# Two transformer layers on one core: the turned features' stores move from SyncE's queue to ScalarE's, one pipeline round later

## The chip, the cores and the metric

The kernel runs on one core of a Trainium2 chip. A core has TensorE (matrix products; PE in the profile), VectorE (DVE), ScalarE (ACT), GpSimd (POOL) and SyncE (SP), each with its own queue of instructions that it runs in order, and 16 DMA engines that move data between memory and the core. A transfer is begun by an instruction in one engine's queue: SP's or ScalarE's here. The metric is the device time of one execution in microseconds (us). The time of a kernel is the median of its runs; the profile is one execution, recorded by the hardware.

## The reference, cut to what matters

There are two layers, each an attention block A and a feed-forward block B, in float32, on 2048 rows of width 576, with 32 heads of 18 and a hidden width of 4608:

```python
def A(x):                                   # x is layer-normed, [1, 2048, 576]
    q, k, v = split_heads(x @ wqkv)         # [1, 32, 2048, 18] each
    pq, pk = (einsum("bhsd,hdf->bhsf", a, w_phi) for a in (q, k))
    phi_q = concat([softmax(pq), softmax(-pq)], -1)
    phi_k = concat([softmax(pk), softmax(-pk)], -1)
    kv = einsum("bhsf,bhsd->bhfd", phi_k, v)
    z = einsum("bhsf->bhf", phi_k)
    num = einsum("bhqf,bhfd->bhqd", phi_q, kv)
    den = einsum("bhqf,bhf->bhq", phi_q, z)[..., None] + 1e-6
    return merge_heads(num / den) @ wo

def B(x):                                   # x is layer-normed
    r = maximum(x @ w1 + b1, 0)
    return (r * r) @ w2 + b2

x = x + A(ln(x)); x = x + B(ln(x))
x = x + A(ln(x)); x = x + B(ln(x))
```

## The kernel before, in words

The rows are worked in four blocks of 512 (`TB`), and a block in four tiles of 128 rows (`NT` = 4). Every float32 product is made of three products of rounded parts (hi x hi, lo x hi, hi x lo), so each operand is split: ScalarE copies the rounded part, VectorE or GpSimd subtracts it.

In a layer, sums over all keys are made first; then the blocks go one after the other through query features, attention output and the feed-forward block. The feed-forward of one block (`g_mlp`, names m_0 to m_3 in the profile) fills TensorE and is the main thread. It takes 36 steps, one for each 128 of the hidden columns. A step f of it:

- `first` loads w1 for the step (three transfers on SP, L1159 and twice L244) and w2 (one, L1161), into two buffers each, and splits them: the copies are L1167 (w1) and L1168, L1169 (w2) on ScalarE, the subtractions L1171, L1174 on VectorE and L1175 on GpSimd.
- `hidden` is 14 matmuls into the tile ph (L1190).
- `square` is L1197 to L1199 on ScalarE (ReLU with the bias, and the square twice) and L1200 on VectorE.
- `second` for the step before, f - 1, is 12 matmuls (L1217) and 3 (L1208).

While this runs, the next blocks' attention is woven in. `weave(main, other, rate)` gives the other thread `rate` units after each step of the main one, and every step of the other thread yields its cost in units. The rate is 3.7 beside the first feed-forward block of a layer and 5.0 beside the second. `chained` orders the steps of the other thread on VectorE, ScalarE and GpSimd one behind the other, and `held` puts them behind the latest square (key "squared", L1199 on ScalarE) and the latest low part (key "last", L1200 on VectorE). Apart from such orders, the place of an instruction in its engine's queue is planned when the program is built.

The features of a block's queries are made in `g_features`, a pipeline over the four tiles: in round i stage k works on tile i - k, the last stage first. The stages are `start` (maximum and minimum, differences), the exponential (ScalarE, 1.15 us), `add` (sums, products with the key sums), `factors`, the scaling (VectorE and GpSimd), and `turn`, which turns 32 x 32 squares in place on VectorE (L897) and begins four transfers on SP (L900), one for each quarter of 32 partitions, to a DRAM tile `home` that holds the features by columns. A transfer moves 144 KB in runs of 32 numbers (128 bytes). Six calls are made in the run, three in each layer: they appear as tiles a_0Q0e to a_3Q3e and the DRAM tiles a_0ft to a_3ft.

`g_out` fetches the turned features back (`fetch`, L928 on SP, 504 KB for a group of heads), into buffers of the tag "E", of which there are four, the same that hold the feature tiles. ScalarE copies (L941) and VectorE subtracts (L942), and TensorE multiplies with the key sums (pn, L964). In four of the six calls another block's queries and features lie between `g_features` and its `g_out`. In the two others (tiles a_1, beside m_2, and a_2 in the second layer, beside m_0) `g_out` follows at once, behind a pause of 5.0 units.

Of the kernel before, what the change touches and what calls it, by code (L numbers as in the profile page):

```python
# [21 lines left out]
def layers_kernel(  # L22
# [18 lines left out]
    nc = tc.nc  # L41
# [77 lines left out]
    def pipeline(n, stages, costs):  # L119

        for i in range(n + len(stages) - 1):
            for k in reversed(range(len(stages))):
                if 0 <= i - k < n:
                    stages[k](i - k)
                    yield costs[k]
# [514 lines left out]
    def soft_parts(src, name, apart=False):  # L640
        if apart:
            e = sb.tile([P, 2 * D], F32R, tag="hb", name=f"{name}e").bitcast(F32)
            e = e.rearrange("p (s d) -> p s d", s=2)
        else:
            e = sb.tile([P, 2, D], F32, tag="E", name=f"{name}e", bufs=4)
        v = src.rearrange("p (h d) -> p h d", d=DH)
        mm = sb.tile([P, 2, H], F32, tag="mm", name=f"{name}m")
        nc.vector.tensor_reduce(mm[:, 0], v, op=ALU.max, axis=AX.X)
        nc.vector.tensor_reduce(mm[:, 1], v, op=ALU.min, axis=AX.X)
        e4 = e.rearrange("p s (h d) -> p s h d", d=DH)  # L650
        m = mm.unsqueeze(3).to_broadcast([P, 2, H, DH])
        dense["parted"] = nc.vector.tensor_sub(e4[:, 0], v, m[:, 0])
        dense["parted", 1] = nc.gpsimd.tensor_sub(e4[:, 1], m[:, 1], v)
        return e

    def soft_exp(e):
        return nc.scalar.activation(e, e, AF.Exp)

    def soft_sums(e, name):
        r = sb.tile([P, 2, H], F32, tag="r", name=f"{name}r", bufs=4)  # L660
        nc.vector.tensor_reduce(r, e.rearrange("p s (h d) -> p s h d", d=DH), op=ALU.add, axis=AX.X)
        nc.vector.reciprocal(r, r)
        return r
# [142 lines left out]
    def held(gen, keys=("last",)):  # L806

        while True:
            with ExitStack() as behind:
                for key in keys:  # L810
                    behind.enter_context(tc.issue_after(dense[key].ins))
                cost = next(gen, gen)
            if cost is gen:
                return
            yield cost
# [15 lines left out]
    def phi_products(layer, e, name):  # L831
        zb = sums[layer]["zb"]
        ms = [sb.tile([P, D], F32, tag="qk", name=f"{name}{s}", bufs=5) for s in range(2)]
        for s in range(2):
            (nc.gpsimd if s else nc.vector).tensor_mul(ms[s], e[:, s], zb[:, s])
        return ms

    def phi_sums(ms, name):
        u = sb.tile([P, 2, H], F32, tag="u", name=name)
        for s in range(2):  # L840
            nc.vector.tensor_reduce(u[:, s], ms[s].rearrange("p (h d) -> p h d", d=DH), op=ALU.add, axis=AX.X)
        return u

    def phi_factors(u, r):
        nc.vector.tensor_mul(u, u, r)
        nc.vector.scalar_tensor_tensor(u[:, 0], u[:, 0], DEN_EPS, u[:, 1], op0=ALU.add, op1=ALU.add)
        nc.vector.reciprocal(u[:, 1], u[:, 0])
        nc.vector.tensor_mul(r, r, u[:, 1].unsqueeze(1).to_broadcast([P, 2, H]))

    def phi_scale(e, r, which=(0, 1)):  # L850
        for s in which:
            e3 = e[:, s].rearrange("p (h d) -> p h d", d=DH)
            dense[f"scaled{s}"] = (nc.gpsimd if s else nc.vector).tensor_mul(
                e3, e3, r[:, s].unsqueeze(2).to_broadcast([P, H, DH]))
# [24 lines left out]
    def g_features(layer, raws, ph, name):  # L879

        rs, ms = {}, {}

        def start(t):
            ph.append(soft_parts(raws[t], f"{name}Q{t}"))

        def add(t):
            rs[t] = soft_sums(ph[t], f"{name}Q{t}")
            ms[t] = phi_products(layer, ph[t], f"{name}m{t}")

        def factors(t):  # L890
            phi_factors(phi_sums(ms.pop(t), f"{name}u{t}"), rs[t])

        turned[name] = home = dram.tile([2 * D, TB], F32, name=f"{name}ft")

        def turn(t):
            flat = ph[t].rearrange("p s d -> p (s d)")
            nc.vector.transpose(flat, flat)  # L897
            for i in range(NQ):
                at = t * P + 32 * i
                nc.sync.dma_start(home[:, at : at + 32].rearrange("(j f) r -> f j r", f=32),  # L900
                                  flat[32 * i : 32 * i + 32].rearrange("f (j r) -> f j r", r=32))

        yield from held(pipeline(NT, (start, lambda t: soft_exp(ph[t]), add, factors, lambda t: phi_scale(ph[t], rs[t]),
                                      turn), (2.6, 0.4, 3.0, 2.8, 1.2, 1.6)), ("last", "squared"))

    def g_out(layer, b, ph, dst, name, parts=1, pause=None, behind=None, norm=None, mid=None, costs=(None, None), o_first=None):

# [793 lines left out]
    def g_attend(layer, b, x, raws, dst, name, behind=None, norm=None, mid=(None, None), ph=None):  # L1701

        if ph is None:
            ph = []
            if raws is None:
                raws = []
                yield from g_queries(layer, b, x, raws, name)
            yield from g_features(layer, raws, ph, name)
        yield 5.0
        if mid[0]:  # L1710
            yield from mid[0]
        yield from g_out(layer, b, ph, dst, name, behind=behind and (behind["last"],), norm=norm, mid=mid[1],
                         costs=(1.0, None if norm else 3.0))
# [120 lines left out]
    for layer in range(2):  # L1834
# [5 lines left out]
        def back_first():  # L1840
            m, later = f"a{layer}_{order[2]}", []
            mid = (g_queries(layer, order[2], None, later, m), g_features(layer, later, early, m))
            yield from g_attend(layer, order[1], None, raws, nxt, f"a{layer}_{order[1]}", dense, None, mid)
# [142 lines left out]
```

## Time and profile before

| | us |
|---|---|
| median of 3 runs | 2439.97 |
| lowest and highest run | 2436.8 and 2958.45 |
| profiled execution | 2442.47 |
| its span in the trace | 2440.8 |
| TensorE busy | 2412.5 |
| VectorE busy | 1560.7 |
| ScalarE busy | 1290.9 |

The profiled execution's time is 1.7 us above its span: that much lies outside the first and last instruction. How to read the lines: "L900" is a line of the kernel; "x4" is a count of instructions; "out<-in" names the tiles written and read, with the numbers of the buffers left out; SPq is SP's queue, and a DMA_DIRECT2D there is the instruction that begins a transfer, whose duration is that of the beginning alone and not of the moving. Such instructions are not counted as busy time of an engine. In a timeline a row has the start, the duration and the engine, and in brackets how long the engine stood before it, and for whom. In a row of waits stand the total, the number and the longest. PEclk is the clock that TensorE was granted, as a share of full speed. The DMA share is the mean busy share of the 16 DMA engines; it can come out a little above 1. A matmul's duration overlaps that of the next: the pace is read from starts.

### The profile page before, as it was taken

Reading aid. Unit: us, or ns where it says so; the run is one execution under the profiler, and the core shown is the slowest. Engines: PE = TensorE matmul, PEld = TensorE weight load, DVE = VectorE, ACT = ScalarE, POOL = GpSimd, SP = SyncE. Lnnn points to the kernel's source line nnn. Section 1 sums busy time; section 2 is a strip of 40 time slices with the busy share of each in tenths; the row PEclk is TensorE's granted clock in tenths of the full one; section 3 lists DMA queues with packets and bytes.
Section 4 is the critical chain, followed back from the end, with each engine's and each line's share of the span. In section 5 each row is a group of like instructions: output and inputs, shape, how many; then the busy total and the mean of one; then the engine's idle time right before and its main releaser. Section 6 shows DMA issues by size and latency. Waiting matters only on the chain. (4 is left out here: it accounts for less than half of the span.)

```text
span 2440.8 us, 41473 instructions
## 1 busy us (share of the span) xinstructions
PE 2412.5 (99%) x14806; PEld 2140.8 (88%) x14806; DVE 1560.7 (64%) x2537; ACT 1290.9 (53%) x2543; POOL 939.9 (39%) x1121
## 2 busy tenths in 40 slices
PE   9999999999999999999999999999998999999999
PEld 8999888888788888888999988888887888888898
DVE  7778848664866655545766788486557675555443
ACT  4344555444446766664433445554455466676643
POOL 4555303222326565542433442032122455565321
PEclk9999999999999999999999999999999999999999
DMA  9124573756654533338753156637667444333364
GB/s 338 64 84 164 163 194 102 168 185 228 151 159 129 162 105 108 112 102 301 254 188 147 59 167 145 173 96 195 194 224 162 130 143 144 119 103 117 110 199 130
DMA packets 370646, 379.40 MB, mean 155 GB/s; under 512 B 142886, under 2 KB 270790, under 8 KB 367878
## 3 DMA queue, kind: packets, MB, share of 16 engines
q1 hardware_dynamic: 369180, 375.37, 51.3%
q8 instruction: 116, 1.90, 0.3%
q10 hardware_dynamic: 1258, 1.37, 0.2%
q14 instruction: 92, 0.75, 0.1%
HBM read 297.22 MB, written 79.41 MB: 154 GB/s over the span
## 5 line engine op out<-in xcount | busy, mean ns | idle before, releaser
L1508 POOL TENSOR_TENSOR m_ps<-m_pr,m_ps 128x128 fp32r<-128x128 f32 x144 | 98.8, 686 | 338.1 <-ACT m_ps L1506 310.9
L1507 DVE TENSOR_TENSOR m_ps<-m_pr,m_ps 128x448 fp32r<-128x448 f32 x144 | 99.8, 693 | 176.1 <-ACT m_ps L1505 176.0
L1550 PE MATMUL m_pacc<-m_ps,m_phb 128*128 128x448 f32 x864 | 185.6, 363 | 0.0
L1550 PEld LDWEIGHTS m_pacc<-m_ps,m_phb 128*128 128x128 f32 x864 | 161.9, 188 | 15.1
L1550 PE MATMUL m_pacacc<-m_ps,m_phc 128*128 128x448 f32 x648 | 147.1, 365 | 0.0
L1505 ACT ACTIVATE m_ps<-m_pr 128x448 fp32r<-128x448 f32 x144 | 82.8, 575 | 115.8 <-issue 66.6
L1550 PEld LDWEIGHTS m_pacacc<-m_ps,m_phc 128*128 128x128 f32 x648 | 119.2, 188 | 7.7
L1190 PE MATMUL m_2ph<-a_2nh,m_2h 128*128 128x512 f32 (+1 forms) x380 | 98.1, 385 | 1.9 <-ACT m_2h L1167 1.7
L1190 PE MATMUL m_0ph<-a_0nh,m_0h 128*128 128x512 f32 (+1 forms) x380 | 97.6, 383 | 1.8 <-ACT m_0h L1167 1.7
L1217 PE MATMUL m_2acc<-m_2s,m_2hb 128*128 128x448 f32 x432 | 95.4, 368 | 2.9 <-ACT m_2s L1168 2.6
L1217 PE MATMUL m_0acc<-m_0s,m_0hb 128*128 128x448 f32 x432 | 95.2, 368 | 2.9 <-ACT m_0s L1168 2.6
L1190 PE MATMUL m_1ph<-t1onh,m_1h 128*128 128x512 f32 (+1 forms) x380 | 95.8, 381 | 0.5 <-ACT m_1hr L1197 0.3
L1190 PE MATMUL m_3ph<-t0onh,m_3h 128*128 128x512 f32 (+1 forms) x380 | 95.7, 381 | 0.2 <-DVE t0onh L534 0.2
L1217 PE MATMUL m_3acc<-m_3s,m_3hb 128*128 128x448 f32 x432 | 93.6, 363 | 0.0
L1217 PE MATMUL m_1acc<-m_1s,m_1hb 128*128 128x448 f32 x432 | 93.5, 363 | 0.0
L1217 PEld LDWEIGHTS m_2acc<-m_2s,m_2hb 128*128 128x128 f32 x432 | 82.0, 191 | 11.7 <-ACT m_2s L1168 3.0
L1217 PEld LDWEIGHTS m_0acc<-m_0s,m_0hb 128*128 128x128 f32 x432 | 81.7, 190 | 11.6 <-ACT m_0s L1168 3.0
L1217 PEld LDWEIGHTS m_3acc<-m_3s,m_3hb 128*128 128x128 f32 x432 | 80.7, 188 | 7.9 <-DVE m_3hb L1200 0.4
L1217 PEld LDWEIGHTS m_1acc<-m_1s,m_1hb 128*128 128x128 f32 x432 | 80.7, 188 | 7.8 <-DVE m_1hb L1200 0.3
L1175 POOL TENSOR_TENSOR m_3s<-m_3r,m_3s 128x128 fp32r<-128x128 f32 x36 | 22.3, 620 | 158.2 <-ACT m_3s L1169 147.0
L1175 POOL TENSOR_TENSOR m_1s<-m_1r,m_1s 128x128 fp32r<-128x128 f32 x36 | 22.0, 612 | 156.7 <-ACT m_1s L1169 139.4
L1190 PEld LDWEIGHTS m_1ph<-t1onh,m_1h 128*128 128x128 f32 x380 | 68.8, 188 | 15.3 <-ACT m_1hr L1197 0.7
(2464 smaller groups left out, 7241.0 us busy)
## 6 DMA issues: line engine op xcount, KB each, us to landing
m_pr<-in_B_w SPq DMA_DIRECT2D x144, 288.0 KB
m_pr<-in_B_w SPq DMA_DIRECT2D x72, 256.0 KB
hd<-m_pu SPq DMA_DIRECT2D x72, 256.0 KB
m_pg<-hd SPq DMA_DIRECT2D x72, 256.0 KB
m_3r<-in_B_w SPq DMA_DIRECT2D x36, 288.0 KB
m_2r<-in_B_w SPq DMA_DIRECT2D x36, 288.0 KB
m_1r<-in_B_w SPq DMA_DIRECT2D x36, 288.0 KB
m_0r<-in_B_w SPq DMA_DIRECT2D x36, 288.0 KB
```

The costliest lines, as they stand in the source:

```text
L1175: nc.gpsimd.tensor_sub(s2[:, FC + P : FC + 2 * P], r2[:, R:], s2[:, FC : FC + P].bitcast(F32))
L1190: dense["hidden"] = nc.tensor.matmul(ph[:, cols], a, m, start=(k == 0), stop=(k == len(ops) - 1))
L1217: nc.tensor.matmul(acc[t][:, :R], a[:, rows], m, start=(f == 0 and k == 0), stop=(f == NF - 1 and k == 2))
L1505: nc.scalar.activation(s2[:, RO : RO + R], r2[:, :R], AF.Copy)
L1507: nc.vector.tensor_sub(s2[:, RO + R : RO + 2 * R], r2[:, :R], s2[:, RO : RO + R].bitcast(F32))
L1508: nc.gpsimd.tensor_sub(s2[:, FC + P : FC + 2 * P], r2[:, R:], s2[:, FC : FC + P].bitcast(F32))
L1550: nc.tensor.matmul(accs[b][t][:, :R], a[:, rows], m, start=(g == 0 and k == 0), stop=(g == NF - 1 and k == 2))
```

## The change

The stage `turn` keeps the turning on VectorE. A seventh stage `store` holds the four transfers, which are now begun by ScalarE's queue. Being the next stage of the pipeline, it works on a tile one round after the turning. The cost of the stage `turn`, 1.6 units, is divided into 1.4 and 0.2.

```diff
         def turn(t):
             flat = ph[t].rearrange("p s d -> p (s d)")
             nc.vector.transpose(flat, flat)
+
+        def store(t):
+            flat = ph[t].rearrange("p s d -> p (s d)")
             for i in range(NQ):
                 at = t * P + 32 * i
-                nc.sync.dma_start(home[:, at : at + 32].rearrange("(j f) r -> f j r", f=32),
+                nc.scalar.dma_start(home[:, at : at + 32].rearrange("(j f) r -> f j r", f=32),
                                   flat[32 * i : 32 * i + 32].rearrange("f (j r) -> f j r", r=32))
 
         yield from held(pipeline(NT, (start, lambda t: soft_exp(ph[t]), add, factors, lambda t: phi_scale(ph[t], rs[t]),
-                                      turn), (2.6, 0.4, 3.0, 2.8, 1.2, 1.6)), ("last", "squared"))
+                                      turn, store), (2.6, 0.4, 3.0, 2.8, 1.2, 1.4, 0.2)), ("last", "squared"))
```

## The prediction

> **What bounds the kernel now.** I read the page's table of engines first, then TensorE's own waits, then the timeline around the longest of them.
>
> ```profile
> span 2440.8 us, 41473 instructions
> PE 2412.5 (99%) x14806; PEld 2140.8 (88%) x14806; DVE 1560.7 (64%) x2537; ACT 1290.9 (53%) x2543; POOL 939.9 (39%) x1121
> ...
> q10 hardware_dynamic: 1258, 1.37, 0.2%
> ```
>
> TensorE is the bound: 28 us of the span are left idle. q10 is ScalarE's queue, almost unused (packets, MB, share). The waits of TensorE, longest first (total, times, longest; the first load is left out):
>
> ```profile
> PE m_2acc L1217 <- ACT m_2s L1168: 2.6, 1, 2.6
> PE m_0acc L1217 <- ACT m_0s L1168: 2.6, 1, 2.6
> PE a_1pn L964 <- ACT a_1fh L941: 2.0, 1, 2.0
> PE m_2ph L1190 <- ACT m_2h L1167: 1.7, 1, 1.7
> PE m_0ph L1190 <- ACT m_0h L1167: 1.7, 1, 1.7
> PE a_2pn L964 <- ACT a_2fh L941: 1.6, 1, 1.6
> ```
>
> They are two copies of one event, once in m_2 and once in m_0, where TensorE stands for copies of weights (L1168, L1167) and of turned features (L941). The timeline of m_0 (start, duration, engine):
>
> ```profile
> 1840.29 0.34 SPq L1161 DMA_DIRECT2D m_0r<-in_B_w  x1
> ...
> 1842.30 0.38 SPq L1159 DMA_DIRECT2D m_0r<-in_B_w  x1
> ...
> 1846.21 0.58 ACT L1168 ACTIVATE m_0s<-m_0r 128x448 fp32r<-128x448 f32 x1 [0.65 <-PE m_0acc L1208]
> ...
> 1847.45 0.80 DVE L1171 TENSOR_TENSOR m_0h<-m_0r,m_0h 128x640 fp32r<-128x640 f32 x1
> ...
> 1849.35 0.69 ACT L1197 ACTIVATE m_0hr<-m_0ph,b1t 128x512 f32<-128x512 f32 x1 [2.36 <-PE m_0ph L1190]
> 1849.55 0.68 DVE L1200 TENSOR_TENSOR m_0hb<-m_0hr,m_0hb 128x512 fp32r<-128x512 f32 x1
> ...
> 1852.25 1.31 PE L1190 MATMUL m_0ph<-a_0nh,m_0h 128*128 128x512 f32 x5
> ...
> 1854.41 2.31 SPq L900 DMA_DIRECT2D a_2ft<-a_2Q1e  x4
> ...
> 1855.43 2.57 PE L1217 MATMUL m_0acc<-m_0s,m_0hb 128*128 128x448 f32 x12
> ...
> 1856.82 0.61 SPq L1161 DMA_DIRECT2D m_0r<-in_B_w  x1
> ...
> 1858.54 1.31 PE L1190 MATMUL m_0ph<-a_0nh,m_0h 128*128 128x512 f32 x5
> ...
> 1861.45 1.38 DVE L897 STREAM_TRANSPOSE a_2Q3e<-a_2Q3e 128x1152 f32<-128x1152 f32 x1
> ...
> 1863.24 3.49 SPq L900 DMA_DIRECT2D a_2ft<-a_2Q3e  x4
> ...
> 1866.78 0.72 SPq L1159 DMA_DIRECT2D m_0r<-in_B_w  x1
> ...
> 1871.65 1.43 PE L1190 MATMUL m_0ph<-a_0nh,m_0h 128*128 128x512 f32 x5 [1.66 <-ACT m_0h L1167]
> ```
>
> A step of m_0 lasts 1858.54 - 1852.25 = 6.29 us, and each should load w2 (L1161) and w1 (L1159) once. Instead SP stands at the store L900 for VectorE's turning, and the next loads start 16.5 us (1840.29 to 1856.82) and 24.5 us (1842.30 to 1866.78) after the last. The copy at 1847.45 had freed the w1 buffer by 1848.25, so the load could have gone then. TensorE's next step starts after 1871.65 - 1858.54 = 13.11 us: 6.8 lost. The step behind it, in TensorE's own timeline:
>
> ```profile
> 1874.95 2.57 PE L1217 MATMUL m_0acc<-m_0s,m_0hb 128*128 128x448 f32 x12
> ...
> 1878.06 0.40 PE L964 MATMUL a_2pn<-a_2fh,kbh 126*126 126x512 f32 x1
> 1878.29 0.40 PE L964 MATMUL a_2pn<-a_2fh,kbl 126*126 126x512 f32 x1
> ...
> 1887.80 2.57 PE L1217 MATMUL m_0acc<-m_0s,m_0hb 128*128 128x448 f32 x12
> ```
>
> From 1874.95 to 1887.80 are 12.85 us for one step and twelve a_2pn matmuls at 0.23: 6.29 + 2.8 = 9.1 by rights, so 3.8 more are lost. Together 10.6 us in m_0. m_2 has the same waits and 0.4 more at L964: I take 11.0. That is 21.6 us in all, the most that this edit can win: in the other four calls of the feature pipeline TensorE does not wait.
>
> **The change, part by part.** *The stores leave SP.* 96 transfers (six calls, four tiles, four quarters). What SP stood there for (total, times, longest), and what the DMA engines did meanwhile (columns: five engines, clock, DMA share, GB/s):
>
> ```profile
> SPq L900 <- DVE a_0Q1e L897: 20.4, 2, 10.7
> ...
> SPq L900 <- DVE a_2Q1e L897: 16.0, 2, 9.7
> ...
> SPq L900 <- DVE a_1Q1e L897: 8.0, 1, 8.0
> ...
> SPq L244 <- DMA a_2w<-a_2ft: 4.0, 3, 2.0
> ```
>
> ```profile
> core 0: us, PE busy (x) PEld busy (x) DVE busy (x) ACT busy (x) POOL busy (x), PEclk, DMA share, GB/s
> 1846.00:1856.00 10.00, 10.00 (x47) 8.57 (x46) 9.90 (x16) 3.61 (x7) 3.92 (x3) 1.00 0.35 58
> 1856.00:1886.00 30.00, 23.82 (x91) 18.74 (x91) 15.90 (x25) 13.69 (x27) 4.12 (x5) 0.89 1.02 216
> 638.00:650.00 12.00, 12.00 (x58) 10.37 (x57) 11.90 (x18) 5.20 (x9) 3.92 (x3) 1.00 0.50 78
> 652.00:682.00 30.00, 23.39 (x89) 18.52 (x88) 14.74 (x22) 14.93 (x29) 3.43 (x5) 0.89 1.00 228
> ```
>
> While SP stood, the DMA engines were partly idle: 10 x (1 - 0.35) = 6.5 us in m_0, 12 x (1 - 0.50) = 6.0 in m_2. Behind that they were full for 30 us, and that is where TensorE lost its time. Loads that no longer stand behind L900 can fill the idle 6.5 and 6.0, no more: the stores' bytes still have to pass in the full stretch. So I count 12.5 us gained, not 21.6. The ends are 0 (the loads do not come forward) and 21.6.
>
> The Trainium skill ("Trainium Kernel Development and Optimization", Key Constraints) says that transfers begun by SP and by ScalarE share the same 16 DMA engines, and that issuing from several engines saves the sequencer's issue time alone. This speaks against the change; the two full rows agree on the sharing, but the rows before them show a wait in front of the issue, for which the rule has no place. What it would leave is the first rival.
>
> *The stores come later.* Between turning and store of the last tile lies a cost of 1.4, at 5.0 per step in these two stages: 0.28 x 6.29 = 1.8 us. Until now SP began 0.4 us after the turning (1861.45 + 1.38 to 1863.24). The fetch of the features waits for all stores, and once the weights are in time the first a_2pn is what comes next: without the lost 6.8 us TensorE would reach it at 1878.06 - 6.8 = 1871.3, only 8.5 us after the last turning ends (1862.83), and store, fetch and copy all lie in between. So I count these 1.8 us in full in both stages, between 0 (the store goes as early as before) and 4.2 (it stands behind the tile before it too, 2.4). It costs 3.6 in all. A tile's buffer, too, comes free with its store, so that the next user of the four buffers (a later tile, or a fetch) waits as much longer; a fetch waits for the stores anyhow, and this is the same term. GpSimd's queue is not passed: it begins no transfer here and its multiplications keep their place.
>
> *ScalarE issues.* What an issue takes now (ns, least, median, most), on SP, and the few that ScalarE has:
>
> ```profile
> L900 SPq DMA_DIRECT2D a_2ft<-a_2Q3e x8: 326/614/1729, 311.6 to 1866.1; - x8
> ...
> L900 SPq DMA_DIRECT2D a_3ft<-a_3Q0e x4: 349/661/2569, 1630.8 to 1634.5; - x4
> ```
>
> ```profile
> L315 ACTq DMA_DIRECT2D wf<-ff x5: 326/357/502, 11.7 to 30.7; - x5
> ```
>
> The pattern is that of L900, not of wf, so I take 0.61 each and 2.4 us a tile, between 1.4 and 10. In its step ScalarE idles 0.65 + 2.36 = 3.0 us (1846.21 and 1849.35), which holds 2.4. If not, what stands behind is the squaring (L1197 to L1199) and the weight copies; TensorE asks for the squares only at 1855.43, 5.2 us after they were done (1849.55 + 0.68). So 3.0 + 5.2 = 8.2 us a tile are covered, and the cost is nothing. Without this cover it is 16 x 0.61 = 9.8 us a call, 59 in all.
>
> The Trainium skill ("Perfetto Trace Analysis", DMA Instruction — HWDGE) has the sequencers share one descriptor generator under a lock, so that ScalarE's issues would queue behind SP's. No run so far shows both at once. By it I would double the 2.4 us a tile, which the cover still holds.
>
> *One more round.* 1.6 becomes 1.4 + 0.2, so the paced sum per tile is unchanged; VectorE's work is the same. Nothing.
>
> Sum against the profiled execution, 2442.47 us: minus 12.5 plus 3.6 is 2433.6. It lies 2.5 above the median of the runs, 2439.97, so against that median **2431**.
>
> **Rivals.** First, *the wait moves to the fetch*. SP now stands at the fetch (L928) for stores that come later, with the weight loads behind it, as L244 does already (4.0 us in the row above, on a transfer that it does not read). The full DMA engines speak for it. If store and issue come 4.2 us later in both stages and what they push back eats most of the 12.5, 0 to 5 us are left: 2435 to 2440, say 2438.
>
> Second, *ScalarE becomes the queue that stands*. Slower. If its order puts a store ahead of the squares and the turning is as late as SP saw it, ScalarE stands 8.0 to 10.7 us plus 2.4, against a cover of 8.2: 2.2 to 4.9 late, say 3.5 in each of six calls, 21 us. It decides as soon as a stand is over 5.8 us. Nothing of the gain is left then if m_0 and m_2 stand as well: 2461; with only some calls late, from 2445. For it: VectorE is busy 9.90 of 10 us, so turnings are late. Against it: the store lies a round behind the turning, and only the last two tiles have little between.
>
> Third, *all comes back*: the loads spread so well that the full stretch goes, and the 21.6 with it: 2418.
>
> Fourth, the edit reorders the queues elsewhere, since their order is planned over the whole program: either way, without a bound.
>
> **Numbers.** The forecast has 0.42 (2425 to 2436 by itself: both stages' stores 2.4 later than counted, or 6 us more of the 21.6 won), the first rival 0.25, the second 0.17, the third 0.13, the fourth 0.03. About half of the second and most of the third belong in a range of 2416 to 2453. A change under 2% (49 us) cannot be told from none here. Faster by more is out of reach of all that TensorE waits for in these stages (21.6), so 0.02 from the fourth; slower by more needs about 8 us late in each of six calls, 0.04; within 0.94.
>
> **What would show it.** L900 on ScalarE's queue, L1159 and L1161 of m_0 and m_2 starting every 6.3 us through the calls; the DMA share of 1846 to 1856 up from 0.35; TensorE's waits on L1168 and L1167 gone, the one on L941 left or grown. Steps of 6.29 us with TensorE waiting on hb or hr (L1197 to L1200) during the calls would prove the second rival, a longer wait of SP at L928 or L244 the first. I am wrong if the two weight waits are gone and the time has not moved, or if they stand unchanged.

## The result and the profile after

The changed kernel takes 2473.59 us, the median of 4 runs (2470.78 to 2477.41), beside 2440.12 for the kernel before, one of whose four runs was slowed, to 2958.45 us, and is left out of the ratio. The ratio, of the runs and not of the two medians, is 1.0143, with a 95% interval of 1.013 to 1.0155: 33.5 us slower, where 9 us faster was forecast, and 20 above the upper end of the range, 2453. The prediction held that under 49 us no change can be told from none; this interval leaves none out. The profiled execution took 2471.94 us. Its page (span, busy time of each engine, and ScalarE's queue with packets, MB and share of the 16 DMA engines):

```profile
span 2470.1 us, 41479 instructions
...
PE 2420.2 (98%) x14806; PEld 2143.4 (87%) x14806; DVE 1563.0 (63%) x2537; ACT 1285.8 (52%) x2543; POOL 938.2 (38%) x1121
...
q10 hardware_dynamic: 113386, 15.53, 3.9%
```

The span grew by 29.3 us. TensorE's idle time went from 2440.8 - 2412.5 = 28.3 to 2470.1 - 2420.2 = 49.9, which is 21.6 of it; the other 7.7 are matmuls, the same in number, that took longer. Line numbers are those of the changed kernel from here on: the stores are L903, the copies L1170 (w1), L1171 and L1172 (w2), `hidden` is L1193, the ReLU L1200, the squares L1201 to L1203, `second` L1220 and L1211, and w1 and w2 are loaded at L1162 and L1164. TensorE's waits (total, times, longest):

```profile
PE m_1ph L1193 <- ACT m_1hr L1200: 9.4, 5, 3.7
PE m_3ph L1193 <- ACT m_3hr L1200: 9.3, 4, 4.0
PE m_0ph L1193 <- ACT m_0hr L1200: 7.6, 3, 3.6
PE m_2ph L1193 <- ACT m_2hr L1200: 7.5, 3, 3.5
...
PE a_1pn L967 <- ACT a_1fh L944: 1.9, 1, 1.9
PE a_2pn L967 <- ACT a_2fh L944: 1.4, 1, 1.4
```

The four waits for the copies of weights in m_2 and m_0 (2.6, 2.6, 1.7 and 1.7, together 8.6) are gone. New are fifteen waits of `hidden` for the ReLU, 33.8 us, in all six calls of the feature pipeline; before, TensorE did not wait in four of them. The net of these rows is 25.2.

SP does what the change was to let it do. Its timeline in m_0 (start, duration, engine):

```profile
1855.53 0.39 SPq L1162 DMA_DIRECT2D m_0r<-in_B_w  x1
...
1863.59 0.39 SPq L1162 DMA_DIRECT2D m_0r<-in_B_w  x1
...
1870.18 0.39 SPq L1162 DMA_DIRECT2D m_0r<-in_B_w  x1
```

One w1 load starts in every step, 8.1 and 6.6 us apart here, where 24.5 us lay between two of them before. So the loss is not there but on ScalarE. Its timeline in the first call, beside m_3:

```profile
305.24 4.30 ACTq L903 DMA_DIRECT2D a_2ft<-a_2Q1e  x4
312.37 0.58 ACT L1171 ACTIVATE m_3s<-m_3r 128x448 fp32r<-128x448 f32 x1 [6.55 <-PE m_3acc L1211]
...
313.05 0.67 ACT L1200 ACTIVATE m_3hr<-m_3ph,b1t 128x512 f32<-128x512 f32 x1
...
314.96 4.20 ACTq L903 DMA_DIRECT2D a_2ft<-a_2Q2e  x4
319.25 3.59 ACTq L903 DMA_DIRECT2D a_2ft<-a_2Q3e  x4
322.95 0.58 ACT L1171 ACTIVATE m_3s<-m_3r 128x448 fp32r<-128x448 f32 x1 [7.42 <-DMA a_2ft<-a_2Q3e]
...
323.63 0.67 ACT L1200 ACTIVATE m_3hr<-m_3ph,b1t 128x512 f32<-128x512 f32 x1
```

And TensorE's, in the same stretch:

```profile
311.43 0.86 PE L1211 MATMUL m_3acc<-m_3hb,m_3s 128*128 128x512 f32 x3
313.77 1.45 PE L1193 MATMUL m_3ph<-t0onh,m_3h 128*128 128x512 f32 x5 [1.49 <-ACT m_3hr L1200]
...
324.35 2.31 PE L1193 MATMUL m_3ph<-t0onh,m_3h 128*128 128x512 f32 x5 [3.97 <-ACT m_3hr L1200]
326.46 1.80 PE L1193 MATMUL m_3ph<-t0onl,m_3h 128*128 128x512 f32 x4
```

Two kinds of loss are to be seen here. First, the stores of the last two tiles stand back to back: eight issues, from 314.96 to 322.84, in front of the ReLU. A step is 6.29 us, so the ReLU behind the one at 313.05 was due at 319.34; it came at 323.63, 4.3 late, and TensorE stood 3.97 for it. So it is in four of the six calls; in the two others (a_0 beside m_3, a_3 beside m_1) the last tile is stored alone. Second, from the stores on the w2 copies run one step ahead. In an undisturbed step the ReLU follows `hidden`, beside `second`, and the w2 copy comes behind it, once `second` has left its buffer. Here the copy lies ahead of the ReLU: at 312.37 it starts when L1211 is done (311.43 + 0.86 = 312.29), the ReLU stands behind it, and TensorE, with `second` over, has nothing to do until the ReLU has read `ph`: 1.49 in the row, or 1.65 counted from where its pace would have put the next start (311.43 + 3 x 0.23 = 312.12). The waits called 1.65 or 1.7 in the expectations are these rows of 1.49.

Why TensorE waits for the ReLU at all is in the code: `ph` has one buffer. `hidden` of the next step writes it, and may begin when the ReLU has read it, long before the squares are needed.

How long the issues took (ns, least, median, most):

```profile
L903 ACTq DMA_DIRECT2D a_2ft<-a_2Q1e x8: 309/1006/1698, 305.2 to 1886.8; - x8
```

That holds more than one kind. Of the 96 issues on ScalarE, 59 began within 0.15 us of the end of the one before them, and took 1.01 us in the middle; the 37 others took 0.31. On SP, before the change, 76 stood in such a row, at 0.64, and 20 did not, at 0.33.

There is a third kind. In m_2 ScalarE stood inside one tile's stores:

```profile
650.00 0.36 ACTq L903 DMA_DIRECT2D a_1ft<-a_1Q0e  x1
...
656.05 1.02 ACTq L903 DMA_DIRECT2D a_1ft<-a_1Q0e  x2
657.25 0.58 ACT L1171 ACTIVATE m_2s<-m_2r 128x448 fp32r<-128x448 f32 x1 [6.53 <-DVE a_1Q3r L662]
```

The releaser that the last row names is not the cause: the queue stood at the third store, whose tile had been turned long before. The program's own order says what that store waits for (number in ScalarE's order, line, tiles, semaphores):

```
644 L903 DMA a_1ft<-a_1Q0e 32x36x32 [waits DVE_49]
647 L903 DMA a_1ft<-a_1Q0e 32x36x32 [waits DMAHW6_49]
648 L903 DMA a_1ft<-a_1Q0e 32x36x32 [waits DMAHW0_49]
...
```

The program gives the transfers of SP and ScalarE eight completion semaphores in turn, and an issue waits until the transfer that had its semaphore last has landed. For the store at 656.05 that was the w1 load that SP began only here, and the sixteen increments of its semaphore (DMAHW0) landed between 655.66 and 656.03:

```profile
653.21 0.38 SPq L1162 DMA_DIRECT2D m_2r<-in_B_w  x1
```

So ScalarE stood 5.3 us for a load of SP's, begun in the meantime. The same is found at 462.56 (3.6 us), 466.51 (3.0), 472.30 (2.2), 1686.70 (3.2), 1690.68 (3.0), 1696.51 (2.2) and 1880.24 (5.4), and for 1.2 to 1.3 at 661.38 and 1885.57.

By what stands in front of the late ReLU, the 33.8 us part into four sums: the four waits behind eight issues in a row (3.97, 3.52, 3.73 and 3.56) are 14.8, the four of 1.49 behind the early copy 6.0, the four behind a stand for a semaphore (2.51 and 2.52 in m_2 and m_0, 3.40 and 3.44 behind the tiles stored alone, whose four issues take another 4.5 us there) 11.9, and three short ones 1.2.

### The profile page after: what moved, and what is told of

Read it like the earlier page. It is cut to its first block, busy times and chain, and to the rows that moved or that the text cites. A ratio compares the mean times of both kernels' runs of the same rounds, so it can differ in the third digit from the quotient of the medians.

```text
span 2470.1 us, 41479 instructions
## 1 busy us (share of the span) xinstructions
PE 2420.2 (98%) x14806; PEld 2143.4 (87%) x14806; DVE 1563.0 (63%) x2537; ACT 1285.8 (52%) x2543; POOL 938.2 (38%) x1121
## 5 line engine op out<-in xcount | busy, mean ns | idle before, releaser
L1193 PE MATMUL m_1ph<-t1onh,m_1h 128*128 128x512 f32 (+1 forms) x380 | 99.3, 391 | 9.8 <-ACT m_1hr L1200 9.4
L1193 PE MATMUL m_3ph<-t0onh,m_3h 128*128 128x512 f32 (+1 forms) x380 | 98.3, 388 | 9.5 <-ACT m_3hr L1200 9.3
L1193 PE MATMUL m_2ph<-a_2nh,m_2h 128*128 128x512 f32 (+1 forms) x380 | 99.0, 388 | 7.7 <-ACT m_2hr L1200 7.5
L1193 PE MATMUL m_0ph<-a_0nh,m_0h 128*128 128x512 f32 (+1 forms) x380 | 98.2, 385 | 7.8 <-ACT m_0hr L1200 7.6
L1193 PEld LDWEIGHTS m_1ph<-t1onh,m_1h 128*128 128x128 f32 x380 | 70.5, 193 | 26.7 <-ACT m_1hr L1200 12.0
L1220 PE MATMUL m_3acc<-m_3s,m_3hb 128*128 128x448 f32 x432 | 93.6, 363 | 0.0
L1220 PE MATMUL m_1acc<-m_1s,m_1hb 128*128 128x448 f32 x432 | 93.5, 363 | 0.0
L1220 PE MATMUL m_0acc<-m_0s,m_0hb 128*128 128x448 f32 x432 | 93.4, 363 | 0.0
L1220 PE MATMUL m_2acc<-m_2s,m_2hb 128*128 128x448 f32 x432 | 93.4, 363 | 0.0
L1193 PEld LDWEIGHTS m_3ph<-t0onh,m_3h 128*128 128x128 f32 x380 | 69.8, 191 | 25.7 <-ACT m_3hr L1200 11.1
L1193 PEld LDWEIGHTS m_2ph<-a_2nh,m_2h 128*128 128x128 f32 x380 | 69.0, 192 | 22.1 <-ACT m_2hr L1200 8.8
L1220 PEld LDWEIGHTS m_1acc<-m_1s,m_1hb 128*128 128x128 f32 x432 | 80.9, 188 | 7.9 <-DVE m_1hb L1203 0.3
L1220 PEld LDWEIGHTS m_0acc<-m_0s,m_0hb 128*128 128x128 f32 x432 | 80.8, 188 | 7.9 <-DVE m_0hb L1203 0.3
L1220 PEld LDWEIGHTS m_2acc<-m_2s,m_2hb 128*128 128x128 f32 x432 | 80.7, 188 | 8.0 <-DVE m_2hb L1203 0.3
L1220 PEld LDWEIGHTS m_3acc<-m_3s,m_3hb 128*128 128x128 f32 x432 | 80.7, 188 | 7.8 <-DVE m_3hb L1203 0.4
```

Source lines behind the costliest of these rows:

```text
L1193: dense["hidden"] = nc.tensor.matmul(ph[:, cols], a, m, start=(k == 0), stop=(k == len(ops) - 1))
L1220: nc.tensor.matmul(acc[t][:, :R], a[:, rows], m, start=(f == 0 and k == 0), stop=(f == NF - 1 and k == 2))
```

## Experiments

The experiments' times are medians beside runs of the kernel before on the same chip, which had medians of 2439.1 to 2440.0 there. My theory after the result: ScalarE's queue is what costs, through (a) the time of the issues, (b) the order around them, and (c) the semaphores; SP is freed as forecast. The rival: the later round delays the features, or the freed loads crowd the DMA engines.

### The later round alone: stores stay with SP

```diff
-                nc.scalar.dma_start(home[:, at : at + 32]...
+                nc.sync.dma_start(home[:, at : at + 32]...
```

> The store is its own stage, one round behind the turning, but SP begins it. If ScalarE's part is what costs (its issues, or the order in its queue), TensorE's waits for the ReLU go and the time is that of the kernel before or a little less, 2428 to 2442 us. If the later round is what costs, the time stays near 2470.

It took 2440.38 us, ratio 1.0007 (0.9998 to 1.0016). TensorE's longest waits:

```profile
PE m_0ph L1193 <- ACT m_0h L1170: 6.4, 1, 6.4
PE m_2ph L1193 <- ACT m_2h L1170: 5.4, 1, 5.4
```

The later round is not the loss. On SP it gathers the two weight waits of each stage into one, at the same time of the whole. Of the rival's other half, the freed loads, this run says nothing, since SP's loads still come late here; against it stands that the changed kernel has no wait for weights left.

### ScalarE alone: stores in the stage of the turning

```diff
             nc.vector.transpose(flat, flat)
-
-        def store(t):
-            flat = ph[t].rearrange("p s d -> p (s d)")
             for i in range(NQ):
...
-                                      turn, store), (2.6, 0.4, 3.0, 2.8, 1.2, 1.4, 0.2)), ("last", "squared"))
+                                      turn), (2.6, 0.4, 3.0, 2.8, 1.2, 1.6)), ("last", "squared"))
```

> ScalarE begins the transfers, but in the stage of the turning, not a round later. If ScalarE's part costs, the time is that of the changed kernel or more, 2465 to 2500, since ScalarE now also stands for VectorE's turning. If the later round costs, it goes back to about 2440.

It took 2488.51 us, ratio 1.0203 (1.0186 to 1.022): 49 us slower than before. The waits are again those of `hidden` for the ReLU, up to 6.8 long. The queue is the loss, and the later round of the change gives back 15 us of it.

### The change in the two calls only that `g_out` follows at once

```diff
+    def g_features(layer, raws, ph, name, late=False):
...
+                (nc.scalar if late else nc.sync).dma_start(home[:, at : at + 32]...
...
+            yield from g_features(layer, raws, ph, name, norm is not None and behind is None)
```

> The change is made only in the two calls that g_out follows at once (beside m_2 and m_0), where TensorE stood for weights before; the four others store from SP in the stage of the turning, as before. If the loss sits in every call where ScalarE stores, the four others (about 27 us of TensorE's lost time in the changed kernel) are back to nothing lost, and the two lose about 3 and 1 us more than before: 2441 to 2447. If moving the stores had helped the two stages by themselves, the time would be under 2430.

It took 2446.19 us, ratio 1.0023 (1.0014 to 1.0033). In four calls nothing is changed, and there TensorE does not wait. In the two others:

```profile
PE m_0ph L1199 <- ACT m_0hr L1206: 7.4, 3, 3.5
PE m_2ph L1199 <- ACT m_2hr L1206: 7.2, 3, 4.2
```

14.6 of new waits less the 8.6 that are gone is 6.0, and 6.2 were measured (2446.19 against 2439.99). So the gain fits the waits that TensorE had, and even in the two calls where there was something to gain the new waits are larger.

### Shorter issues: the same bytes in 32 runs of 4608 bytes

```diff
+            block = home.rearrange("a b -> (a b)").rearrange("(p d) -> p d", d=2 * D)
...
-                nc.scalar.dma_start(home[:, at : at + 32].rearrange("(j f) r -> f j r", f=32),
-                                  flat[32 * i : 32 * i + 32].rearrange("f (j r) -> f j r", r=32))
+                nc.scalar.dma_start(block[at : at + 32], flat[32 * i : 32 * i + 32])
```

> As the changed kernel, but each of the 96 transfers writes its 32 rows as whole rows of 4608 bytes: the same bytes from the same queue in the same order, in 32 long runs instead of 1152 short ones. The features then lie in the wrong order in DRAM, so the output is not the reference's; what is left out is the order alone. If the time of an issue (0.6 to 1.7 us each for most) is what holds up the ReLU, issues fall to about 0.3 us and the loss goes: about 2426 to 2435, with the weights in time. If the planned order (the w2 copy, which stands for TensorE, ahead of the ReLU) is what costs, the waits of about 1.7 us stay, two or three a call: about 2446 to 2460.

It took 2450.67 us, ratio 1.0053 (1.0038 to 1.0068): two thirds of the loss are gone. The issues, the last tile of the first call on ScalarE, and ScalarE's queue on the page:

```profile
L904 ACTq DMA_DIRECT2D a_2ft<-a_2Q1e x8: 309/450/913, 307.7 to 1873.2; - x8
```

```profile
321.10 1.89 ACTq L904 DMA_DIRECT2D a_2ft<-a_2Q3e  x4
```

```profile
q10 hardware_dynamic: 5866, 15.53, 1.9%
```

Four issues take 1.89 us, where the same four took 3.59. The waits for the ReLU fall to 23.1 us in all, in a profiled execution that was 5 us above the median. The order on ScalarE is that of the changed kernel, and the four waits of 1.49 in m_2 and m_0 stay. So the time lies in the second range expected, and yet most of the loss was the issues' length. In this run and the others with runs of 4608 bytes the kernel leaves out the order of the features in DRAM, so they show what a transfer costs and not a kernel that could be used.

### The ReLU first: w2 copies and low parts behind the squares

```diff
-            nc.scalar.activation(s2[:, RO : RO + R], r2[:, :R], AF.Copy)
-            nc.scalar.activation(s2[:, FC : FC + P], r2[:, R:], AF.Copy)
+            def copies():
+                nc.scalar.activation(s2[:, RO : RO + R], r2[:, :R], AF.Copy)
+                nc.scalar.activation(s2[:, FC : FC + P], r2[:, R:], AF.Copy)
+
+            if not defer:
+                copies()
...
             square(f)
+            if later:
+                with tc.issue_after(dense["squared"].ins):
+                    later.pop()()
```

> As the changed kernel, but the copies and subtractions of the next step's w2 stand behind the squares of this step, so that no w2 copy stands ahead of the ReLU behind a store. If the order is what costs, all waits for the ReLU go and the time is 2426 to 2436. If the time of the issues costs, only the four waits of 1.7 us go and those of 3.6 to 4.1 behind the last two stores of a call stay: 2458 to 2468.

With the stores of the change it took 2458.73 us, ratio 1.0083 (1.0068 to 1.0098): 15 us less than the changed kernel, in the second range expected. The waits of 1.49 are mostly gone, those at the end of the six calls are left, 2.0 to 3.5 long. ScalarE's and TensorE's timelines at the first of them:

```profile
312.94 0.36 ACTq L903 DMA_DIRECT2D a_2ft<-a_2Q2e  x1
...
317.63 3.14 ACTq L903 DMA_DIRECT2D a_2ft<-a_2Q3e  x4
320.82 0.69 ACT L1208 ACTIVATE m_3hr<-m_3ph,b1t 128x512 f32<-128x512 f32 x1 [7.21 <-DMA a_2ft<-a_2Q3e]
```

```profile
321.56 2.50 PE L1201 MATMUL m_3ph<-t0onh,m_3h 128*128 128x512 f32 x5 [2.53 <-ACT m_3hr L1208]
```

Eight issues lie in front of the ReLU, from 312.94 to 320.77, and TensorE waits 2.53 of these 7.83 us: 5.3 are covered. In the same call of the second layer it is 7.33 and 2.02, again 5.3.

> Both edits at once: long runs of 4608 bytes (the features lie in the wrong order in DRAM; the order alone is left out) and the w2 copies behind the squares. If the time of the issues and the planned order are all there is, no wait for the ReLU over 1 us is left, and with the weights in time 2422 to 2432. If ScalarE also stands for transfers of SP that use the same completion semaphore, waits of 2 to 3.5 us stay in some calls (before the third transfer of the first store beside m_2 and m_0, within the third store of the second call of a layer): 2434 to 2446.

With the wide stores as well it took 2435.73 us, ratio 0.9983 (0.9974 to 0.9993). Shorter issues and order are worth 23 and 15 us alone and 38 together: the two costs add up. Two waits for the ReLU of 4.0 and 3.4 are left in m_0 and m_2, where ScalarE still stands about 3 us for a semaphore.

> The kernel before the change with the w2 copies and low parts put behind the squares, the stores left with SP. If the order alone is worth nothing while ScalarE begins no transfers: 2437 to 2443. If it is a gain by itself, of up to the 15 us seen between the two kernels with the stores on ScalarE: 2425 to 2435. If w2 comes late through it: above 2445.

The control, this order with the stores left with SP as before the change, took 2440.78 us, ratio 1.0003 (0.9994 to 1.0012). The order is worth nothing while ScalarE begins no transfers; it only repairs what the stores did.

### One issue for each tile

```diff
-            for i in range(NQ):
-                at = t * P + 32 * i
-                nc.scalar.dma_start(block[at : at + 32], flat[32 * i : 32 * i + 32])
+            whole = home.rearrange("a b -> (a b)").rearrange("(p d) -> p d", d=2 * D)
+            nc.scalar.dma_start(whole[t * P : (t + 1) * P], flat)
```

> As the one with both edits, but a tile is stored by one transfer of 128 rows in place of four of 32: a quarter of the issues and of the completion semaphores that ScalarE can stand for. If the semaphores matter, it is faster than that one by 5 to 12 us, at 2422 to 2432; if not, the two agree within 4 us.

With the ReLU first it took 2421.95 us, ratio 0.9924 (0.9907 to 0.994). No wait for the ReLU is left. It is 13.8 us faster than with four wide issues, more than the 5 to 12 expected of the semaphores alone, and with the stands the rest of the row of issues went too.

> The changed kernel with one transfer of 128 rows of 4608 bytes for each tile in place of four (the order of the features in DRAM is left out), and the order of the w2 copies as the change has it. If the copy that the plan puts ahead of the ReLU costs by itself, whatever the issue lasts, the 15 us between the two kernels with four wide transfers (2450.67 and 2435.73) come back on the 2421.95 of the one with a single transfer: 2434 to 2438, with waits of hidden for the ReLU of about 1.65. If the order costs only where a long or a standing issue lies in front of it, 2421 to 2426 with no such wait.

Without that order it took 2423.96 us, ratio 0.9936 (0.9923 to 0.995), the second of the two cases. ScalarE's timeline in the first call:

```profile
295.51 0.33 ACTq L902 DMA_DIRECT2D a_2ft<-a_2Q0e  x1
296.79 0.58 ACT L1169 ACTIVATE m_3s<-m_3r 128x448 fp32r<-128x448 f32 x1 [0.65 <-PE m_3acc L1209]
...
299.92 0.69 ACT L1198 ACTIVATE m_3hr<-m_3ph,b1t 128x512 f32<-128x512 f32 x1 [2.36 <-PE m_3ph L1191]
...
301.80 0.33 ACTq L902 DMA_DIRECT2D a_2ft<-a_2Q1e  x1
```

With one issue of 0.33 us ScalarE has the same idle times of 0.65 and 2.36 as without any, and a step still lasts 6.29 us (295.51 to 301.80). The plan moves no copy ahead of the ReLU either: the bad order comes with four issues in a row, not with a store as such. One issue for each tile, with wide runs, is free on ScalarE; four are not.

> As the run that took 2421.95 (one wide transfer for each tile, the w2 copies behind the squares; the order of the features in DRAM is left out), but the transfer is begun by SP in the stage of the turning, as before the change. If that gain is that SP no longer stands for VectorE's turning, it is gone here: 2436 to 2442, with TensorE's waits of 2.6 and 1.7 on the w2 and w1 copies back in m_2 and m_0. If it is that the transfer is cheaper for the DMA engines, it stays: 2419 to 2426.

The same single transfer on SP, in the stage of the turning, took 2426.4 us, ratio 0.9945 (0.9932 to 0.9957): the first case expected did not come, the second by 0.4 us not quite, and most of the gain stays without leaving SP. SP's timeline in m_0:

```profile
1844.51 0.34 SPq L899 DMA_DIRECT2D a_2ft<-a_2Q1e  x1
1845.22 0.40 SPq L1157 DMA_DIRECT2D m_0r<-in_B_w  x1
...
1850.77 0.33 SPq L899 DMA_DIRECT2D a_2ft<-a_2Q2e  x1
1851.48 0.38 SPq L1157 DMA_DIRECT2D m_0r<-in_B_w  x1
```

The loads (L1157) now start 6.3 us apart between the stores. SP no longer shows a wait for the turning at the store, and its order came out otherwise, with loads of weights between any two stores, where before the stores of one tile followed on those of the other. The narrow transfer also costs the DMA engines more: q10 had 3.9% of the span in the changed kernel and 1.9% with wide runs, for the same bytes. So this run cannot part a cheaper transfer from a better order on SP; it does show that SP's stand can go without another queue.

### The stores behind the loads on SP

```diff
+            with tc.issue_after(traced_on(nc.sync)):
                 for i in range(NQ):
...
+                    nc.sync.dma_start(home[:, at : at + 32]...
```

> The kernel before the change with the four stores put behind the latest load that was traced on SP, so that a load of weights would not stand behind a store. If the weight loads are traced ahead of the stores and this frees them: 2420 to 2430 and the waits of 2.6 and 1.7 gone. If what stands behind the store are loads traced later, which this order does not reach: 2438 to 2442 with the same waits.

It took 2440.53 us, ratio 1.0001 (0.9993 to 1.001), with the waits of 2.6 in place, which is the second case: this order does not reach the loads that come late.

### GpSimd begins the stores

```diff
-                nc.scalar.dma_start(home[:, at : at + 32]...
+                nc.gpsimd.dma_start(home[:, at : at + 32]...
```

> The changed kernel with the transfers begun by GpSimd's queue, which neither loads weights nor makes the ReLU. If all of the loss is ScalarE's queue, it is gone, and with SP free of the stores the weights are in time: 2420 to 2436. If GpSimd is slow at beginning such transfers, its part of the low halves of w2 (620 to 690 ns each, one a step) comes late to TensorE: above 2445.

It took 2467.65 us, ratio 1.0117 (1.0102 to 1.0132). The issues, and GpSimd's timeline behind the last tile of m_0:

```profile
L903 POOL DMA_DIRECT2D a_2ft<-a_2Q3e x8: 817/819/828, 323.1 to 1904.1; - x8
```

```profile
1901.65 3.25 POOL L903 DMA_DIRECT2D a_2ft<-a_2Q3e  x4 [8.86 <-DVE a_2Q3e L897]
1904.91 0.51 POOL L1178 TENSOR_TENSOR m_0s<-m_0r,m_0s 128x128 fp32r<-128x128 f32 x1
```

The stand for the turning moves along with the stores: GpSimd stands 8.86 us, with the low parts of w2 (L1178) behind it. TensorE waits 6.1 and 6.0 for copies of w2 in m_2 and m_0. That these come from GpSimd's stand is not shown: in m_0 GpSimd was done with the last of these low parts at 1906.79, and SP began the next load of w2 only at 1918.59. SP, ScalarE and GpSimd each have work behind the stores that TensorE needs.

### How many issues in one place

The single issue was also a wide one. To part the two, the narrow transfer was kept and the number in one place changed.

```diff
             nc.vector.transpose(flat, flat)
+            quarters(t, nc.sync, range(2))

         def store(t):
+            quarters(t, nc.scalar, range(2, NQ))
...
+        def quarters(t, queue, which):
...
+            for i in which:
```

> As the changed kernel, but two of a tile's four stores are begun by SP with the turning, as before the change, and two by ScalarE one round later. If the loss goes with the number of issues that lie together on ScalarE, it falls by half or more: 2440 to 2455, with the longest wait for the ReLU, at the last two tiles, at about half of 3.6. If any narrow store on ScalarE costs as much, through the copy that is planned ahead of the ReLU: 2460 to 2474. SP stands for the turning again, so the waits of 2.6 and 1.7 in m_2 and m_0 can be back.

Two on each queue took 2459.33 us, ratio 1.008 (1.0062 to 1.0099): 43% of the loss gone, between the two cases expected. No wait for the ReLU is over 2.0 now, but most are still the 1.49 of the order, and the features come later (waits of 4.2 and 3.8 for a_1fh and a_2fh).

> As the kernel with half of the stores on each queue, with the w2 copies and low parts put behind the squares. If the planned order makes what is left of the loss: 2432 to 2440, at or under the kernel before. If it is the issues' own time: as the kernel without this, within 3 us.

With the ReLU first as well, 2451.71 us, ratio 1.0049 (1.0033 to 1.0065): the order is worth 7.6 us here, and neither expectation holds; single waits of 2.2 to 3.7 for the ReLU and the later features are left. I did not follow these.

```diff
-                                      turn, store), (2.6, 0.4, 3.0, 2.8, 1.2, 1.4, 0.2)), ("last", "squared"))
+                                      turn, *(lambda t, i=i: store(t, (i,)) for i in range(NQ))), (2.6, 0.4, 3.0, 2.8, 1.2, 1.4, 0.05, 0.05, 0.05, 0.05)), ("last", "squared"))
```

> As the changed kernel, but the four stores of a tile lie in four stages of the pipeline, one round apart and 0.05 units each, so that where the rounds are long each round holds at most one issue of a tile, and up to four of different tiles at the end. If the count of issues in one place is what costs: 2440 to 2460, with waits only behind the last tile. If it is the transfer of 128-byte runs itself: 2465 to 2480, waits spread over more steps.

One issue for each tile and round took 2489.55 us, ratio 1.0203 (1.0188 to 1.0218), slower than either expectation. ScalarE's and TensorE's timelines show why:

```profile
296.24 0.34 ACTq L903 DMA_DIRECT2D a_2ft<-a_2Q0e  x1
...
302.52 0.32 ACTq L903 DMA_DIRECT2D a_2ft<-a_2Q0e  x1
...
322.69 1.67 ACTq L903 DMA_DIRECT2D a_2ft<-a_2Q3e  x2
324.46 0.58 ACT L1171 ACTIVATE m_3s<-m_3r 128x448 fp32r<-128x448 f32 x1 [11.20 <-DMA a_2ft<-a_2Q3e]
```

```profile
325.86 2.50 PE L1193 MATMUL m_3ph<-t0onh,m_3h 128*128 128x512 f32 x5 [6.12 <-ACT m_3hr L1200]
```

The stages were spread, the issues were not: the first stand alone, and the last thirteen in a row, from 312.63 to 324.36. But the run answers the question. A narrow issue that stands alone takes 0.32 to 0.34 and leaves the step at 6.28 us (296.24 to 302.52), like the wide one; in a row most take 0.7 to 0.8, some up to 1.5, and TensorE waits 6.12, in other calls up to 9.7. So a narrow store is free on ScalarE as well, as long as it stands alone; in a row the issues cost by their number and by their length there.

## Why the prediction was wrong

**What bounds the kernel: right.** The waits for weights in m_2 and m_0 came from SP's standing at the stores, and they went when the stores left SP.

**The stores leave SP, minus 12.5: right in kind, the size not shown.** The loads came forward as described. The waits that went are 8.6 us, and the run with two calls changed agrees (14.6 - 8.6 against 6.2); read from starts, as the prediction read its 6.8 in m_0, the same two places are 13.6. Up to 18 us were there (2421.95 against 2440), but with another transfer, and no run has the term alone. The sign that went with it did not come: in the changed kernel the stretch in which VectorE is busy (1858 to 1870, 11.93 of 12) has a DMA share of 0.28. With one issue for each tile on ScalarE it is 0.78 in 1846 to 1856, and 0.79, no longer 1.02, in the 30 us behind.

That the two full rows agree with the shared DMA engines is misread: ScalarE began no transfer in either stretch, so they say nothing of it.

**The stores come later, plus 3.6: not seen.** The later round alone is at 1.0007, from 0.5 us faster to 3.9 slower, so 3.6 is just not excluded; in the changed kernel the waits for the first turned features are 1.9 and 1.4, where they were 2.0 and 1.6.

**ScalarE's issues, nothing: this step failed.** The sentence was that 3.0 + 5.2 = 8.2 us a tile are covered, and so the cost is nothing. In its place the runs show fifteen waits of `hidden` for the ReLU, 33.8 us. Four things were wrong with it.

The cover was too large. The 5.2 were read from the squares, for which TensorE asks late. But ahead of the squares in ScalarE's queue stands the ReLU, which `hidden` needs to get its one buffer back. The rows that show it stood in the prediction: the ReLU at 1849.35 lasts until 1850.04, and `hidden` begins at 1852.25, right behind `second`. So the ReLU can come 2.2 us late and not 5.2, and the cover is 3.0 + 2.2 = 5.2, as the run with the ReLU first measured it (5.3).

An issue in a row was not 0.61 but 1.01 in the middle, so that four in one place take 3.1 to 4.5 instead of 2.4. In four of the six calls the last two tiles fall into one step, 7.5 to 7.9 us against the cover of 5.2; at 2.4 a tile the two would have been covered, with 4.8. And the program with transfers on ScalarE has another order, the w2 copy ahead of the ReLU, and other stands, those at shared semaphores. A sign of the last stood in the prediction too, SP's wait at L244 for a transfer that it does not read: there, as well, the transfer had used its semaphore before.

The rule that issues from SP and ScalarE queue at one descriptor generator (the Trainium skill, "Perfetto Trace Analysis", DMA Instruction — HWDGE) would have given 4.8 us a tile, nearer to the 3.1 to 4.5 than my 2.4. The runs do not show its lock, though: the four issues at 319.25 took 3.59 us while SP began nothing, as its timeline in the changed kernel has it:

```profile
315.66 1.17 SPq L244 DMA_DIRECT2D m_3r<-in_B_w  x2
324.52 0.33 SPq L1164 DMA_DIRECT2D m_3r<-in_B_w  x1
```

The same section counts the making of the descriptors into an issue's recorded time. With that the runs agree: 1,152 runs of 128 bytes against 32 of 4608 is 1.006 against 0.450 in the middle for the tile a_2Q1e. The number of runs is not all of it: the same issue took 0.31 where none stood right before it, and in a row 0.64 on SP, 1.01 on ScalarE, and 0.66 on ScalarE in the run without the later round. Why these differ stays open.

**One more round, nothing: right** by the first experiment.

**The rivals.** The second had the right side and the right queue. Its end of 2461 was too low, because it counted with the same cover of 8.2, and its mechanism was another: ScalarE stood not for the turning but for its own issues, for a copy that waits for TensorE, and for SP's transfers. The first rival's sign, a longer wait of SP at the fetch, is there in part: SP's waits at L931 for the transfers of a_1w and a_2w are 4.3 and 3.3, where they were 1.5 and 0.7 at L928. But it did not reach TensorE, whose waits for the first features are 1.9 and 1.4. The third, all comes back (21.6), is near what one issue for each tile reaches, 18.

**From waits to time.** The listed waits give a net of 25.2 us, the idle time rose by 21.6 (short waits elsewhere went too; I did not follow them), and matmuls that lasted longer add 7.7. TensorE slows down behind a long wait: five matmuls of `hidden` took 2.31 after the wait of 3.97 and 1.45 after the one of 1.49, against 1.31 before the change. The granted clock was 0.57 and 0.52 in the stretches of the nine matmuls behind the long wait (324.3 to 326.4 and 326.4 to 328.1), and 1.00 before and after. The prediction's sum had no term for this, although its 6.8 and 3.8, read from starts, hold the same cost. The Trainium skill ("Perfetto Trace Analysis", Matmul Optimizations) has TensorE scale its power with its use; the trace agrees, by these clocks.

What stays open is how much of the 33.8 belongs to the semaphores. No more than 11.9 lie behind a stand for one, and part of these is the issues' own time; the run with one issue for each tile takes away the row of issues, the order and the stands together, and no run changes the semaphores alone.

## What to carry to other kernels

Before a transfer is moved to another engine's queue, find the first instruction behind it that the bounding engine needs, and what that instruction frees: the cover reaches only that far, not to the next result that is asked for late. Count the issues that will lie in one place, with their duration in a row, and first try to make them fewer: one issue for each tile was free on ScalarE and nearly as good on SP (in kernels that leave out the order of the features), four on ScalarE made the kernel 33 us slower. Where an order is planned and completion semaphores are shared, a moved transfer also brings a new order and waits for the other queue's transfers, so look at the order of the new program before its time.

## What the runs showed of the hardware

An issue of a transfer in runs of 128 bytes took 0.31 to 0.34 us where none stood right before it; in a row it took 1.01 in the middle on ScalarE and 0.64 on SP, up to 2.1 and 2.6. In runs of 4608 bytes it took 0.31 to 0.45 in the middle, by tile, and on GpSimd, in runs of 128 bytes, 0.82 nearly each time. What stood behind it in its queue did not start meanwhile: the copy behind the issues of 319.25 to 322.84 began at 322.95. An issue also stood until the transfer that had used its semaphore before had landed, whichever queue had begun that one: 655.66 to 656.03 for the increments, 656.05 for the store. And a wait costs TensorE more than its length: behind the one of 3.97 the next nine matmuls took 2.31 and 1.80 us instead of 1.31 and 1.07, or 1.7 us more.
